# One product for numerators and denominators of tiles 8 to 15, a freer choice of engines, and smaller loads, in a planned transformer-block kernel

## The chip, the cores and the metric

The kernel runs on one core of one Trainium2 chip. A core has five engines that run their own instruction streams and meet at semaphores: TensorE (PE in the profile; PEld is its weight load), VectorE (DVE), ScalarE (ACT), GpSimd (POOL) and SyncE (SP), which here only issues DMAs. The metric is the device time of one execution in microseconds; the median of several executions is compared.

## The reference

One block with adaptive layer norms, an attention in linear form and a gated MLP, on 2048 tokens of width 512. What matters of it:

```python
def _A_ref(x, wqkv, w_phi, wo):           # 32 heads of 16
    pq, pk = q @ w_phi, k @ w_phi          # per head
    phi_q = concat([softmax(pq), softmax(-pq)])
    phi_k = concat([softmax(pk), softmax(-pk)])
    kv = einsum('bhsf,bhsd->bhfd', phi_k, v)
    z = einsum('bhsf->bhf', phi_k)
    num = einsum('bhqf,bhfd->bhqd', phi_q, kv)
    den = einsum('bhqf,bhf->bhq', phi_q, z)[..., None] + 1e-06
    return (num / den) @ wo
def _B_ref(x, w_gate, w_up, w_down):       # 1376 wide
    return (sigmoid(x @ w_gate) * (x @ w_up)) @ w_down
h = layernorm(x) * (1 + ca) + sa;  x = x + ga * _A_ref(h)
h = layernorm(x) * (1 + cb) + sb;  x = x + gb * _B_ref(h)
```

The six vectors sa to gb come from silu(c) @ w_mod.

## The kernel before, in words

The 2048 tokens are 16 tiles of 128. In the first part the kernel takes the statistics of every tile (bn_stats, L897 and L898), normalises it (xn, L923 to L927), transposes it on PE (tp_h, L941) or by a transposing DMA (L933), and applies the modulation (hm1, L948 and L950). K and V products (L968, L972) follow per tile; ScalarE takes exponentials of both signs (L984), VectorE sums and inverts them (L987, L1000), GpSimd multiplies (phi, L990), and PE adds phi times V into two accumulators (kvacc, L458). The column of ones in V makes the sums z beside kv. From the accumulators come block-diagonal matrices kvbd of 144 columns for each of 8 groups: 128 for the numerators, 8 for z and 8 for the plain sums of exponentials of the queries.

The second part works on units of one or two query tiles (UNITS). The queries' exponentials eT (L1047) lie transposed and not normalised. For a unit, sm (L553) multiplies eT by the last 16 columns of kvbd, 8 products a tile; smS (L557) copies half of the result, and den (L563 to L566) makes of it the factor cc for each head and sign. Then num (L578) multiplies eT by the first 128 columns, u (L584) scales it by cc, o (L602, GpSimd) adds the two signs, a DMA transposes o (L605), a_ps (L611) multiplies by wo. x1 (L616), its statistics (L620, L621), the second normalisation xn2 (L653 on ScalarE, L655 on VectorE), its transpose (L660) and mod (L675) give the input of the MLP. The MLP runs in chunks of 1, 1, 2, 4, 4 and 4 tiles: for each of 11 slices of the width a gate and an up product (L696), tg (tanh, L700, ScalarE) and hm (L705, VectorE), and then for each tile 11 products y (L719), fin (L728) and a store (L730).

The order is not the order of the program text. Every operation is a task in a graph, with the engines it may run on and their costs, its reads and writes, and its buffers. A list scheduler (order, L240) plays the graph through with these costs and always takes the ready task with the lowest due time; tables DUE, REL and ENG shift the due and release times of single tasks and fix engines. The result is one fixed order for each engine, with a wait wherever a task needs another's result or buffer. Buffers are rings with few places (CAPS, L424): 8 PSUM banks, 2 places for tg, 6 of 2 KB for phi and u, 2 for the inputs of an MLP chunk. Engines take their tasks strictly in the planned order.

Loads go through SP's queue, in planned order too: x in pieces of 2, 2, 4, 4 and 4 tiles (x0a, x0b, x1, x2, x3), the weights wk, wv, wq (512 KB each), w_mod in two pieces of 512 KB and one of 2 MB (wm1), wo, wg, wu, wd (L777 to L793). Before the first data come, PE runs 22 products on zeros (warm, L825).

A second graph behind a branch on a flag (L1124) repeats the work in a safer form for large inputs. With these inputs it is not taken.

Of the kernel before, what the change touches and what calls it, by code (L numbers as in the profile page):

```python
# [9 lines left out]
FP32 = mybir.dt.float32  # L10
# [6 lines left out]
P = 128  # L17
S, D, H, DH, F = 2048, 512, 32, 16, 1376
NT = S // P
KT = D // P  # L20
# [39 lines left out]
TD = [0, 0, 1, 0, 0, 0, 1, 1, 0]  # L60
DUE = {
    "ld_x0a": -97.1, "ld_wm01": 152.0, "ld_x0b": 222.2, "ld_wv": 207.5, "ld_x1": 81.5, "ld_x3": -0.1, "ld_wq": -14.2, "ld_wg": 19.9, "ld_wu": 3.4,
    "ld_wd": -29.9, "c1": 13.0, "c2": 147.3, "c3": 14.4, "scb": 6.0, "bd": 165.0, "pmem": 11.4, "wdz": -3.1, "modc1.0": 26.7, "modc1.1": 19.0,
    "modc1c": 2.7, "modc2.0": 74.4, "tpw0": -20.5, "wTc0": -4.8, "tpw1": -10.4, "wTc1": 7.4, "tpw2": 52.0, "wTc2": 2.1, "wTc3": 23.5, "foldc10": 219.5,
    "fold11": 191.9, "fold12": -0.3, "foldc12": -11.6, "fold13": -5.6, "foldc13": 5.3, "ld_wd2": 13.8, "wqT2": -3.5, "foldc00": -13.3, "fold01": 157.0,
    "foldc01": 0.1, "fold02": -52.2, "fold03": -1.9, "foldc03": 127.5, "st1_0": -0.5, "rs1_0": -0.3, "xn1_0": -6.5, "tph00": 49.2, "hm1_00": 5.6,
    "tph01": -4.8, "hm1_01": 155.9, "tph02": 63.8, "hm1_02": 82.7, "tph03": 34.8, "hm1_03": -1.8, "st1_1": -0.5, "nmr1_1": -5.4, "xn1_1": 112.1,
    "tph10": -23.9, "hm1_10": 3.2, "tph11": -0.8, "hm1_11": -7.3, "tph12": 28.2, "hm1_12": 97.5, "tph13": -14.9, "st1_2": 19.0, "st1_3": 33.1,
    "rs1_2": 32.5, "nmr1_2": 157.2, "xn1_2": -2.3, "xT1_2": 140.7, "xT1_3": 123.5, "hm1_20": 218.8, "hm1_21": -5.3, "hm1_22": -18.5, "hm1_23": -3.9,
    "st1_4": -3.5, "rs1_3": 79.1, "nmr1_3": -1.5, "xn1_4": 105.0, "xn1_5": -0.8, "tph30": -5.2, "hm1_30": -15.4, "tph31": -42.3, "hm1_31": -28.8,  # L70
    "tph32": 41.0, "hm1_32": 152.2, "tph33": -0.5, "hm1_33": 25.8, "st1_6": 162.7, "st1_7": 38.8, "rs1_4": 95.1, "nmr1_4": -2.5, "xn1_6": 219.0,
    "xn1_7": 209.9, "tph40": 160.1, "hm1_40": 104.8, "tph41": -30.3, "hm1_41": 90.7, "tph42": -16.0, "hm1_42": 9.7, "tph43": 140.8, "hm1_43": 56.3,
    "st1_8": -47.7, "st1_9": 172.5, "nmr1_5": 89.8, "tph50": 231.5, "hm1_50": -1.8, "hm1_51": 59.9, "tph52": 175.6, "hm1_52": 231.3, "tph53": -17.7,
    "hm1_53": -12.9, "st1_10": 18.2, "st1_11": 153.1, "rs1_6": -0.5, "nmr1_6": 0.5, "xn1_10": 91.7, "xT1_10": 127.3, "xT1_11": 123.6, "hm1_60": 29.7,
    "hm1_61": -1.0, "hm1_62": 199.8, "hm1_63": 6.2, "st1_12": -7.3, "st1_13": 11.8, "rs1_7": 10.0, "nmr1_7": -15.9, "xn1_12": 87.0, "xn1_13": -20.2,
    "xT1_12": 204.7, "xT1_13": -7.7, "hm1_70": -5.2, "hm1_71": -13.4, "hm1_72": -4.7, "hm1_73": 189.5, "st1_14": 106.3, "st1_15": -14.0, "rs1_8": 14.5,
    "nmr1_8": -9.3, "xn1_15": 108.4, "tph80": 17.5, "hm1_80": -4.7, "tph81": 15.4, "hm1_81": -25.1, "tph82": 14.9, "hm1_82": -4.7, "tph83": 98.2,
    "hm1_83": -4.7, "K0": -4.8, "e0.0": 17.5, "n0.0": 92.8, "r0.0": -1.1, "V0": 141.0, "kv0.0": 14.6, "K1": -21.7, "e1.0": 155.4, "n1.0": 12.9,
    "r1.0": -29.0, "va1": 5.5, "kv1.0": -3.5, "K2": -3.7, "e2.0": -26.5, "n2.0": 5.8, "r2.0": 0.9, "phi2.0": 90.9, "V2": 40.0, "va2": 61.0, "kv2.0": 17.6,
    "K3": -10.3, "e3.0": 141.6, "n3.0": -16.1, "r3.0": -4.1, "phi3.0": 192.3, "V3": 21.9, "va3": 8.8, "kv3.0": -13.1, "K4": 34.7, "e4.0": 10.3,  # L80
    "r4.0": -19.6, "phi4.0": 69.5, "V4": 129.0, "kv4.0": 68.3, "K5": 158.4, "e5.0": -6.7, "n5.0": -0.2, "r5.0": 182.5, "phi5.0": 7.9, "V5": 156.3,
    "va5": 209.5, "kv5.0": 68.4, "K6": 1.8, "e6.0": 11.3, "n6.0": -3.5, "r6.0": -9.4, "phi6.0": 217.5, "V6": 1.0, "va6": 23.6, "kv6.0": -7.7, "K7": -26.2,
    "e7.0": -7.2, "n7.0": -8.8, "r7.0": 27.6, "phi7.0": 32.4, "V7": -6.3, "va7": 99.3, "kv7.0": -15.3, "K8": 2.3, "e8.0": -17.2, "n8.0": 104.1,
    "r8.0": 17.0, "phi8.0": -6.8, "V8": -3.5, "va8": 42.1, "kv8.0": 6.7, "K9": 152.5, "n9.0": -40.0, "r9.0": -2.9, "phi9.0": 87.3, "V9": 0.3, "va9": -14.4,
    "kv9.0": -1.4, "e10.0": 2.6, "n10.0": 83.9, "V10": -10.5, "va10": -24.9, "K11": -1.8, "e11.0": -20.5, "n11.0": 0.3, "r11.0": -2.4, "phi11.0": 8.5,
    "e11.2": 35.6, "r11.2": -38.9, "n11.4": -6.0, "phi11.4": -0.3, "e11.6": -16.4, "r11.6": 248.2, "phi11.6": 5.2, "V11": -11.2, "va11": 131.5,
    "kv11.0": 4.3, "kv11.4": 25.6, "kv11.6": 0.7, "K12": -47.6, "e12.0": -5.7, "r12.0": 0.6, "phi12.0": 28.5, "V12": 22.2, "kv12.0": 0.7, "K13": 0.2,
    "n13.0": 31.7, "r13.0": -2.9, "phi13.0": 11.3, "n13.4": 9.9, "r13.4": -5.2, "phi13.4": 8.1, "V13": 83.3, "va13": 72.9, "kv13.0": 79.9, "kv13.4": -6.7,
    "K14": 83.3, "e14.0": -6.3, "n14.0": 106.6, "r14.0": 116.9, "e14.4": -4.5, "n14.4": 6.8, "r14.4": 0.5, "V14": 161.0, "va14": -8.2, "kv14.0": -20.6,
    "kv14.4": -8.1, "K15": 107.4, "e15.0": 0.1, "n15.0": 0.8, "r15.0": -0.7, "phi15.0": 4.0, "e15.4": -2.9, "n15.4": 0.7, "phi15.4": 8.5, "va15": 60.4,  # L90
    "kv15.0": 78.1, "kv15.4": 15.7, "perm": 45.8, "kvm0": 186.2, "kvm1": -4.0, "kvp0": 3.0, "kvp1": 22.2, "kvp2": -20.5, "kvz0": 67.0, "kvz1": -5.4,
    "kvn1": 119.1, "kvz2": -16.9, "gbc": -29.4, "ga": -9.7, "gac": -2.9, "wo0": -30.7, "wo1": 79.0, "wo2": -42.3, "wo3": -21.1, "wmod_free": 122.0,
    "wd0": -0.5, "wd1": 0.3, "wd2": -0.5, "wd3": 90.8, "wd4": 29.9, "wd5": 0.2, "wd6": 28.7, "wd7": 11.0, "wd9": 7.6, "wd10": 6.8, "Q00": 111.8,
    "qe00": -26.3, "Q01": -2.5, "qe01": 62.0, "Q02": -19.2, "qe02": -2.3, "Q03": 168.0, "Q10": 91.7, "qe10": -13.7, "Q11": 76.2, "qe11": -27.8,
    "Q12": 10.0, "qe12": 86.0, "Q13": -0.5, "qe13": 5.1, "Q20": 2.0, "qe20": 60.8, "qe21": 14.0, "qe22": 106.1, "Q23": -11.0, "qe23": 13.1, "Q30": 78.8,
# [111 lines left out]
class Graph:  # L207
# [948 lines left out]
```

## Time and profile before

| | us |
|---|---|
| median of 9 runs | 220.72 (220.44 to 221.67) |
| profiled execution | 221.19 |
| its span | 219.3 |
| last VectorE operation begins | 213.68 |

The span runs from the first to the last instruction; about 1.9 us of the execution lie around it. In the groups of instructions, "mean ns" is the time of one instruction from start to end. Neighbours on one engine can overlap, so a row of equal instructions takes less than the sum of the means: 16 sm products have a mean of 169 ns each, and follow each other in 24. Therefore the spacing of starts on the timeline is used for PE and VectorE where it is known.

The costliest groups of the part that the change touches:

```profile
L584 DVE TENSOR_TENSOR u<-num,cc 128x512 f32<-128x512 f32 x28 | 18.2, 682 | 0.9 <-PE num L578 0.5
...
L602 POOL TENSOR_TENSOR o<-u 128x512 bf16<-128x512 f32 x14 | 17.5, 1267 | 48.4 <-DVE u L584 35.9 <-ACT tg L700 12.4
...
L578 PE MATMUL num<-kvbd,eT 128*128 128x128 bf16 x128 | 10.4, 219 | 0.0
...
L675 DVE TENSOR_SCALAR wT_sb<-wT_sb,modc 128x256 bf16<-128x256 bf16 x16 | 4.5, 339 | 0.5 <-DMA wT_sb<-xn 0.4
...
L553 PE MATMUL sm<-kvbd,eT 128*128 128x16 bf16 x128 | 4.3, 169 | 0.0
```

The columns after the bar are busy us, mean ns of one, and the idle time of the engine just before, with what ended it.

### The profile page before, as it was taken

How to read it: one execution, taken by the hardware profiler on the slowest of the kernel's cores; microseconds unless marked ns; L12 is line 12 of the kernel's file. 1: busy time of each engine (PE TensorE's matmuls, PEld its weight loads, DVE VectorE, ACT ScalarE, POOL GpSimd, SP SyncE). 2: the span in 40 equal slices, each digit the busy share in tenths (PEclk: the TensorE clock that was granted, in tenths of full speed). 3: DMA queues.
4: the chain of work that ended last, by engine and by line, in shares of the span. 5: the costliest groups of instructions: out<-in, count | busy, mean ns of one | idle time of the engine just before them, and what ended most of it. 6: DMA issues, size and time to landing. Idle time of an engine off the chain costs nothing.

```text
span 219.3 us, 4340 instructions
## 1 busy us (share of the span) xinstructions
PE 205.4 (94%) x1583; PEld 114.7 (52%) x1583; DVE 165.3 (75%) x381; ACT 109.0 (50%) x255; POOL 89.9 (41%) x113
## 2 busy tenths in 40 slices
PE   7986989999899989999999999998999999999990
PEld 2733545464466568867775454553454444444450
DVE  3989899998469998878969777899698854344230
ACT  3789898999769974523630532240332522332100
POOL 4249898999999944521102015340006100000000
PEclk9996999999999999999999999999999999999997
DMA  6995995991000201250431003054002322000021
GB/s 188 364 243 138 334 216 109 346 379 48 0 3 0 43 16 22 49 98 0 51 72 48 27 1 72 1 75 120 0 24 51 72 51 72 0 4 0 27 72 34
DMA packets 31455, 19.02 MB, mean 87 GB/s; under 512 B 21729, under 2 KB 29378, under 8 KB 31426
## 3 DMA queue, kind: packets, MB, share of 16 engines
q1 hardware_dynamic: 30896, 18.65, 33.6%
q8 instruction: 14, 0.23, 0.4%
q14 instruction: 15, 0.12, 0.2%
q10 hardware_dynamic: 530, 0.02, 0.1%
HBM read 11.58 MB, written 2.10 MB: 62 GB/s over the span
## 4 chain that ended last, share of the span: by engine, by line
PE 66%; DMA 12%; DVE 8%; ACT 4%; SPq 3%; POOL 2%; issue 2%; ACTq 0%; POOLq 0%; DVEq 0%
PE u_ps L696 17%; PE g_ps L696 17%; PE y_ps L719 14%; DMA wqk_sb<-in_A_wqkv_dram 5%; PE a_ps L611 4%; PE k_ps L968 4%; PE v_ps L972 3%; DVE u L584 2%; PE num L578 2%; DMA wp_sb<-in_A_w_phi_dram 2%; DMA wqk_sb<-xn 2%; ACT e L984 2%; DMA x_sb<-in_A_x_dram 2%; POOL phi L990 2%; SPq L660 1%
## 5 line engine op out<-in xcount | busy, mean ns | idle before, releaser
L700 ACT ACTIVATE tg<-g_ps 128x512 bf16<-128x512 f32 (+4 forms) x66 | 29.6, 454 | 73.2 <-PE g_ps L696 64.2
L705 DVE SCALAR_TENSOR_TENSOR wmod_sb<-tg,u_ps 128x512 bf16<-128x512 bf16 (+5 forms) x66 | 32.4, 503 | 23.0 <-PE u_ps L696 20.4
L719 PE MATMUL y_ps<-wd_sb,wmod_sb 128*128 128x512 bf16 (+3 forms) x187 | 42.8, 366 | 0.0
L602 POOL TENSOR_TENSOR o<-u 128x512 bf16<-128x512 f32 x14 | 17.5, 1267 | 48.4 <-DVE u L584 35.9
L696 PEld LDWEIGHTS <-wu_sb 128*128 128x128 bf16 (+1 forms) x264 | 23.3, 100 | 17.7 <-issue 0.6
L696 PEld LDWEIGHTS <-wg_sb 128*128 128x128 bf16 (+1 forms) x264 | 23.2, 100 | 17.1
L990 POOL TENSOR_TENSOR phi<-e,ks 128x1024 bf16<-128x1024 bf16 (+2 forms) x22 | 31.5, 1452 | 0.3
L719 PEld LDWEIGHTS <-wmod_sb 128*128 128x128 bf16 (+1 forms) x187 | 17.8, 98 | 15.7
L696 PE MATMUL u_ps<-wT_sb,wu_sb 128*128 128x512 bf16 (+3 forms) x132 | 26.0, 326 | 0.0
L696 PE MATMUL g_ps<-wT_sb,wg_sb 128*128 128x512 bf16 (+3 forms) x132 | 25.5, 326 | 0.0
L696 PE MATMUL u_ps<-wqk_sb,wu_sb 128*128 128x256 bf16 (+5 forms) x132 | 21.3, 290 | 0.3 <-DVE x L616 0.3
L584 DVE TENSOR_TENSOR u<-num,cc 128x512 f32<-128x512 f32 (+1 forms) x32 | 20.7, 682 | 1.0 <-PE num L578 0.5
L696 PE MATMUL g_ps<-wqk_sb,wg_sb 128*128 128x128 bf16 (+5 forms) x132 | 21.2, 290 | 0.0
L987 DVE TENSOR_REDUCE ks<-e 128x64 f32<-128x1024 bf16 (+2 forms) x22 | 19.3, 912 | 0.8 <-ACT e L984 0.8
L728 DVE TENSOR_TENSOR ot<-y_ps,x 128x512 bf16<-128x512 f32 (+1 forms) x17 | 11.1, 656 | 9.8 <-PE y_ps L719 9.6
L984 ACT ACTIVATE e<-k_ps 128x512 bf16<-128x512 f32 (+2 forms) x44 | 18.3, 491 | 0.4 <-PE k_ps L968 0.2
L972 PE MATMUL v_ps<-wv_sb,h1T 128*128 128x512 bf16 x64 | 17.2, 400 | 0.7 <-DVE h1T L950 0.7
L611 PE MATMUL a_ps<-wo_sb,oT 128*128 128x512 bf16 x64 | 16.3, 379 | 1.1 <-DMA oT<-o 1.0
L1047 ACT ACTIVATE eT<-q_ps 128x512 bf16<-128x512 f32 x32 | 16.9, 626 | 0.2 <-PE q_ps L1042 0.2
L968 PE MATMUL k_ps<-wqk_f,h1T 128*128 128x512 bf16 x64 | 16.0, 379 | 0.0
L1042 PE MATMUL q_ps<-h1T,wqk_f 128*128 128x512 bf16 x64 | 15.6, 379 | 0.0
L897 DVE BATCH_NORM_STATS2 st<-x_sb 128x6 f32<-128x512 bf16 x16 | 10.8, 673 | 4.0 <-DMA x_sb<-in_A_x_dram 4.0
(129 smaller groups left out, 276.8 us busy)
## 6 DMA issues: line engine op xcount, KB each, us to landing
wmod_sb<-in_w_mod_dram SPq DMA_DIRECT2D x1, 2048.0 KB, 10.4
out_dram<-ot SPq DMA_DIRECT2D x15, 128.0 KB, 1.7
x_sb<-in_A_x_dram SPq DMA_DIRECT2D x3, 512.0 KB, 6.6
wg_sb<-in_B_w_gate_dram SPq DMA_DIRECT2D x1, 1376.0 KB
wu_sb<-in_B_w_up_dram SPq DMA_DIRECT2D x1, 1376.0 KB, 9.6
wd_sb<-in_B_w_down_dram SPq DMA_DIRECT2D x1, 1280.0 KB, 13.6
wqk_sb<-in_A_wqkv_dram SPq DMA_DIRECT2D x2, 512.0 KB, 7.6
wmod_sb<-in_w_mod_dram SPq DMA_DIRECT2D x2, 512.0 KB, 6.4
```

Source lines behind the costliest of these rows:

```text
L584: dve.tensor_tensor(u[:], ps[:].rearrange("p (h d) -> p h d", d=DH), cc[:, q, s, :].unsqueeze(2).to_broadcast([P, H, DH]), op=ALU.mult)
L602: G.add(f"o{t}", {"POOL": 1.3}, lambda e, ub=ub, o=o: pool.tensor_tensor(o[:], ub[0][:].rearrange("p h d -> p (h d)"), ub[1][:].rearrange( ...
L611: pe.matmul(ap_[:], lhsT=oT[:, j, :], rhs=wo_sb[:, j, :], start=(j == 0), stop=(j == KT - 1))
L696: pe.matmul(ps[:fsz, 0:n], lhsT=w[:, j, ft * P:ft * P + fsz], rhs=h[:, j, 0:n], start=(j == 0), stop=(j == KT - 1))
L700: G.add(f"tg{k}.{ft}", {"ACT": 0.13 + n * 0.00083}, lambda e, tg=tg, g_ps=g_ps, fsz=fsz, n=n: act.activation(tg[:fsz, 0:n], g_ps[:fsz, 0:n ...
L705: dve.scalar_tensor_tensor(hm_all[:fsz, hm[k].slot, ft, 0:n], tg[:fsz, 0:n], 1.0, u_ps[:fsz, 0:n], op0=ALU.add, op1=ALU.mult)
L719: pe.matmul(y[:, 0:c1 - c0], lhsT=hm_all[:fsz, hm[k].slot, ft, tl * P:(tl + 1) * P], rhs=wd_sb[:fsz, ft, c0:c1], start=(ft == 0), stop=(ft ...
L968: pe.matmul(kp[:], lhsT=h1T[:, j, t * P:(t + 1) * P], rhs=wqk_f[:, j, D:2 * D], start=(j == 0), stop=(j == KT - 1))
L972: pe.matmul(vp[:], lhsT=h1T[:, j, t * P:(t + 1) * P], rhs=wv_sb[:, j, :], start=(j == 0), stop=(j == KT - 1))
L984: act.activation(ee[:, ha:hb, s, :], kp[:, ha * DH:hb * DH].rearrange("p (h j) -> p h j", j=DH), ACT.Exp, scale=1.0 - 2.0 * s)
L987: dve.tensor_reduce(ks[:, ha:hb].rearrange("p h s -> p (h s)"), ee[:, ha:hb].rearrange("p h s j -> p (h s) j"), axis=AX.X, op=ALU.add)
L990: pool.tensor_tensor(ph[:, ha * 32:hb * 32].rearrange("p (h j) -> p h j", j=DH), ee[:, ha:hb].rearrange("p h s j -> p (h s) j"), ks[:, ha: ...
```

## The change

It has four parts.

1. For units 5 to 8 (tiles 8 to 15; MGU = 5) the products sm and num become one product with all 144 columns of a group. A tile's 8 groups fill three PSUM banks (groups 0 to 2, 4 to 6, and 3 with 7). Three copies z take the 16 last columns of each group to SBUF, on ScalarE or VectorE; dn makes cc from them, and u is cut in four pieces for each tile. A tile's numerators wait for the cc of the tile before.
2. The planner may choose among more engines: copies between ScalarE and VectorE, o, wo and wd between GpSimd and VectorE, xn2 and mod among three engines. A preference keeps the old engine except where the table ENG names another. In the built order 48 tasks change engine: among them 16 mod tasks leave VectorE (12 to ScalarE, 4 to GpSimd), four xn2 go from ScalarE to GpSimd and one (tile 14) to VectorE, and hm1_71 goes from GpSimd to VectorE.
3. The third piece of w_mod is loaded as three (512 KB, 1 MB, 512 KB), and loads are released at other times. SP's order at the start becomes x0a, wk, x0b, the two w_mod pieces, x1, wv, wq, x2, two transposes, one transpose of wq, x3 (before: x0a, wk, x0b, the two w_mod pieces, wv, x1, x2, wq, two transposes, two transposes of wq, x3).
4. DUE, REL and ENG are new throughout, so the order of all engines is new.

```diff
+            merged = p >= MGU
+            if merged:
+                for q, t in enumerate(tiles):
+                    zS = small("smS", [P, 8, 16])
+                    for i in range(3):
+                        ps = nums[t, i] = bank("num")
+                        gs = range(4 * i, 4 * i + 3) if i < 2 else (3, 7)
+                        def f_num(e, t=t, gs=gs, ps=ps):
+                            for c, g in enumerate(gs):
+                                pe.matmul(ps[:, c * (P + 16):(c + 1) * (P + 16)], lhsT=eT[t // 4][:, g, (t % 4) * P:(t % 4 + 1) * P],
+                                          rhs=kvbd[:, g, :], start=True, stop=True)
...
+                        G.add(f"num{t}{i}", {"PE": 0.0615 * len(gs)}, f_num, r=KVZ + [("kvn", 0), ("kvn", 1), ("kvn", 2), ("cc", t - 1)] + eTk, w=[("num", t, i)],
...
+                        G.add(f"z{t}{i}", {"ACT": 0.24, "DVE": 0.13}, f_z, r=[("num", t, i)], w=[("z", t, i)], bufs=[ps, zS], due=d0 + q, pref=["ACT"])
+                    def f_small(e, zS=zS, m=m, den=den, cc=cc):
+                        zv = zS[:].rearrange("p (s b) n -> p s b n", s=2)
+                        for s in range(2):
+                            dve.tensor_tensor(m[:, 0, s * 32:(s + 1) * 32].rearrange("p (b n) -> p b n", n=8),
+                                              zv[:, s, :, 0:8], zv[:, 1 - s, :, 8:16], op=ALU.mult)
+                        dve.tensor_tensor(den[:, 0], m[:, 0, 0:32], m[:, 0, 32:64], op=ALU.add)
+                        dve.reciprocal(den[:, 0], den[:, 0])
+                        for s in range(2):
+                            dve.tensor_tensor(cc[:, 0, s].rearrange("p (b n) -> p b n", n=8), zv[:, 1 - s, :, 8:16],
+                                              den[:, 0].rearrange("p (b n) -> p b n", n=8), op=ALU.mult)
...
+                    for i in range(3):
+                        for s in (i,) if i < 2 else (0, 1):
+                            nh, h0, c0 = (24, 0, 0) if i < 2 else (8, 24, s)
...
-    load("wm1", ["wmod1"], lambda e: sp.dma_start(wmod_sb[:, :, 1024:3072], wmod_v[:, :, 1024:3072]), 2048 * K1, 30.0, rel=22.0)
+    for nm, c0, c1, due in (("ga", 2, 3, LD[1]), ("m2", 3, 5, LD[2]), ("gb", 5, 6, LD[3])):
+        load("wm" + nm, ["wmod_" + nm], lambda e, c0=c0, c1=c1: sp.dma_start(wmod_sb[:, :, c0 * D:c1 * D], wmod_v[:, :, c0 * D:c1 * D]), (c1 - c0) * 512 * K1, due, rel=due)
...
-                G.add(f"mod{p}{j}", alts, f_mod, r=rr, w=[("h2", p, j)], bufs=bb, due=d0 + 3, port=() if via_pe else ("DVE",))
+                    pf, alts, rr, bb = ["DVE"], {"DVE": 0.27, "ACT": 0.47, "POOL": 0.45}, [("h2raw", t) for t in tiles] + ["mod2"], [h2[k]]
+                G.add(f"mod{p}{j}", alts, f_mod, r=rr, w=[("h2", p, j)], bufs=bb, due=d0 + 3, port=() if via_pe else ("DVE", "POOL"), pref=pf)
```

The f_small here is the dn task: two products, one sum, one reciprocal and two products, six operations of 32 columns.

## The prediction

> **What bounds the kernel now.** I read the page first (shares of the engines and the 40 slices), then windows of 5 us, then the timeline where a window loses time.
>
> ```profile
> span 219.3 us, 4340 instructions
> ...
> PE 205.4 (94%) x1583; PEld 114.7 (52%) x1583; DVE 165.3 (75%) x381; ACT 109.0 (50%) x255; POOL 89.9 (41%) x113
> ...
> PEclk9996999999999999999999999999999999999997
> ```
>
> PE is the bound. The reader should see two things: PE's 6% of idle time and the one dip of the clock in the fourth slice. The windows (columns: stretch, its length, busy time of PE, PEld, DVE, ACT, POOL with counts, granted clock, DMA share, GB/s) say where they lie:
>
> ```profile
> 15.00:20.00 5.00, 2.10 (x13) 0.83 (x12) 4.90 (x14) 3.73 (x11) 4.13 (x5) 0.85 0.55 86
> 20.00:25.00 5.00, 5.00 (x32) 2.52 (x31) 4.12 (x13) 4.24 (x13) 4.21 (x5) 0.81 0.89 243
> ...
> 40.00:45.00 5.00, 5.00 (x44) 2.59 (x42) 4.97 (x7) 5.00 (x11) 4.94 (x9) 1.00 1.03 412
> ...
> 55.00:60.00 5.00, 4.44 (x51) 2.54 (x49) 2.41 (x5) 3.85 (x11) 4.84 (x5) 1.00 0.00 0
> ...
> 115.00:120.00 5.00, 5.00 (x40) 2.51 (x39) 4.63 (x11) 0.43 (x2) 1.27 (x1) 1.00 0.14 40
> ...
> 150.00:155.00 5.00, 3.96 (x19) 1.67 (x18) 3.65 (x8) 0.60 (x1) 0.00 (x0) 1.00 0.38 92
> ```
>
> PE idles 2.9 us at 15 to 20 and works at half clock just after, 0.6 at 55 to 60, 1.0 at 150 to 155; between, 5.00 of 5.00. At 30 to 55 VectorE, ScalarE and GpSimd are full too. The timeline shows what the two large gaps wait for:
>
> ```profile
> 12.73 0.69 DVE L897 BATCH_NORM_STATS2 st<-x_sb 128x6 f32<-128x512 bf16 x1 [0.79 <-DMA x_sb<-in_A_x_dram]
> ...
> 17.05 0.23 PE L941 MATMUL tp_h<-ident,xn 128*128 128x128 bf16 x1 [1.64 <-POOL xn L927]
> ...
> 19.11 1.89 PE L972 MATMUL v_ps<-wv_sb,h1T 128*128 128x512 bf16 x4 [0.75 <-DVE h1T L950]
> ```
>
> ```profile
> 151.85 1.04 PE L611 MATMUL a_ps<-wo_sb,oT 128*128 128x512 bf16 x4 [1.04 <-DMA oT<-o]
> ```
>
> The first is a chain: tokens 512 to 1023 (load x1) land, VectorE takes their statistics, GpSimd normalises, PE transposes. The second is one output product waiting for a transposed o behind SP's queue. The four v matmuls at 19.11 take 1.89 us; four take 0.86 elsewhere in the chain of waits.
>
> **What the Trainium skill says.** "TensorE: Matmul & The Clock Gate", part 1, states that an idle window of 3413 ns halves the clock; here the dip lasts one such window (0.85 and 0.81 granted), so the trace agrees. The same page, "Wait — 56ns, not 53.3ns?", gives a floor of about 25 ns from start to start for small matmuls: the sm products show 0.39 us for 16. "DMA: Bandwidth & Descriptors", [...]its HWDGE ordering part say that one queue's descriptors are consumed in order, so a load moved forward in SP's list lands earlier by the bytes it overtakes. "SBUF — State Buffer", the shared port pair, says that GpSimd and some VectorE forms lock each other out; a VectorE xn at 5.83 us took 1.23 us beside a GpSimd operation, 0.38 at 8.58, which agrees.
>
> **The change, part by part.** Durations are from the profiled execution (span 219.3, its own time 221.19, so 1.9 us lies around the span); the median is 220.72. I apply differences to the median.
>
> 1. One product for tiles 8 to 15. Before, each tile costs PE 8 sm and 8 num products:
>
> ```profile
> 113.01 0.39 PE sm L553 x16
> ...
> 114.06 0.45 PE num L578 x8
> ```
>
> That is 24.4 and 56.2 ns each, 0.645 us a tile. After: 8 products of 144 columns at 56.2 x 144/128 = 63 ns (estimate from the row), 0.506 us. Eight tiles: -1.1 us of PE, in a stage where PE is full. Bounds: -0.8 if short products were partly hidden, -1.5 if 144 columns cost no more than 128.
>
> 2. What it costs VectorE. Before, a pair's den takes from 117.60 to 119.03 on the timeline, 1.43 us, and u 0.60 us from start to start (three in 1.88), four per pair: 1.92 us a tile. After: six small operations on 32 columns. Independent tiny ones follow each other in 0.08 us and dependent ones in 0.19 (timeline at 155.3 to 156.0), a 32-column reciprocal takes 0.353 (group L565): about 1.1. Then u of 384 elements twice (0.47 each, 0.60 scaled, against 0.425 busy for the 256-column ot) and of 128 twice (0.21): 1.36. Together 2.46, +0.54 a tile, +4.3 in all. Six of the 24 z copies go to VectorE (about 0.15 each, +0.9), and xn2 of tile 14 (0.804 mean, +0.7). ScalarE gets 18 z copies at about 0.21 (smS 128x64) against 1.8 us of smS; it is 50% busy, so this is hidden. Against it, 16 mod operations leave VectorE: 0.28 each (eight in 2.22 us), -4.4. Net +1.5 over the kernel, but about +4 inside 115 to 175, where the windows hold 51.4 busy of 60. That fits, at 92%, if it is spread evenly. Bounds for PE: 0 to +0.5 us for each tile. The numerators of a tile now wait for the denominator of the tile before (cc of t-1), and queued behind them on PE are y and gate products; in the built order 2.4 us or more of other PE work (counted at 0.86 us for four products of 512 columns and 0.216 for one) lies between consecutive tiles, against about 3.2 us of VectorE work per tile, fins included. I take +0.3 in all.
>
> 3. Loads. x1 is issued before wv, wq before x2, x3 behind one transposed load instead of two; the 2 MB w_mod load is cut in three. x1 overtakes 512 KB: at the 330 GB/s of window 10 to 15 that is 1.6 us, so it lands near 11.2 instead of 12.7, and wv there instead of 11.2 (7.8 us from its issue). VectorE is free at 11.9, so the statistics of tiles 4 and 5 gain 0.8, and the normalisation after them (two more statistics stand ahead of nmr) about 1.2. The first V product needs wv at 13.31: cover 0.6 us; if that is gone, the same 1.2 is lost again. x2 lands 1.6 us later, near 17, and VectorE reads it after 18. The later w_mod pieces are needed after 40 us; cutting them costs SP two issues of 0.57, between transposes that have slack. Earlier transposes on PE: 1.2 of the 2.9 us.
>
> 4. Engines. In the key stage GpSimd's work from 43.86 is one unbroken run, and its last phi releases PE:
>
> ```profile
> 43.86 16.34 POOL L990 TENSOR_TENSOR phi<-e,ks 128x1024 bf16<-128x1024 bf16 x14
> ```
>
> One hm1 leaves it (0.555). On ScalarE, two fold copies, an hm1 and the two-part reciprocals go to VectorE, while va7, va12 and va13 come: -1.1 us up to the last e. VectorE in exchange gains about +1.4 up to its last reciprocal; its cover is the start, 0.8 to 1.2 earlier, and the 0.77 it waits for ScalarE at 53.95. So the stage can end 1.2 + 0.5 sooner by GpSimd; with VectorE nearly used up I take -1.5 for parts 3 and 4 together (bounds 0 and -2.2).
>
> 5. New order near 150. In the built order tile 12's transposed o stands before y's last 22 products (4.7 us), and needs about 4 (POOL o 1.27, SP issue, 2.4 to landing). The 1.04 gap goes; late next are the modulations of tiles 8 to 11, so -0.7. The tail (last y to end, 5.6 us) keeps its form: a full store before the last half one; 0, at most +0.2. The switch of other copies between ScalarE and VectorE has cover on both: 0.
>
> Sum: -1.1 + 0.3 - 1.5 - 0.7 = -3.0; 220.72 - 3.0 = 217.7.
>
> **Rivals.** (a) The start's gain stays in the start: VectorE, with +1.4 us, ends the key stage where it did, and PE idles at 57 to 60 instead of 16 to 19. For it: 4.97 of 5.00 VectorE at 40 to 45; against: 2.41 at 55 to 60. Then -1.1 + 0.3 - 0.7: 219.2. (b) PE's activity in the window before 18.5 grows enough that the clock is not halved. For: the transposes come 1.2 us earlier; against: even then PE works only some 1.2 of that 3.4 us. The 3.4 us at half speed cost 1.7: 216.0. (c) Slower: the chain product, z copy, small operations, u per tile is longer than the PE work laid between tiles, so PE's in-order queue stands at each tile's numerators, and banks (three per tile instead of two and a shared half) come free late, which holds gate and up products too. Price per tile t; it turns the sign from 3.3/8 = 0.41 us a tile, and at 0.55 gives 220.72 - 3.3 + 4.4 = 221.8. For: VectorE at 92% and six small operations in a row; against: the mods that leave, and PE without idle time from 115 to 150 today. (d) Everything comes out even: 220.7.
>
> **Numbers.** Forecast 217.7 (own range 216.6 to 218.8) 0.47; (a) 219.2 (218.8 to 220.2) 0.16; (b) 216.0 (215.2 to 216.6) 0.14; (c) 221.8 (220.9 to 223) 0.17; (d) 220.7 0.06. A change within 0.2% (0.44 us) can't be told from none: faster 0.47 + 0.16 + 0.14 = 0.77, same 0.06, slower 0.17. The range leaves out most of (c) and the lower end of (b): 215.4 to 220.9.
>
> **What would show it.** Sm products drop from 128 to 64 and num rows show 144 columns at about 63 ns; the first tp_h of tile 4 near 15.9 and a shorter PE gap; the phi run on POOL ending near 58.6; no gap over 0.4 us before out12; PE idle at 115 to 150 under 0.7 us. It is wrong if PE shows waits on dn or u of tiles 8 to 15 of more than 3 us in sum, if V's first product waits for wv, or if VectorE rather than GpSimd ends the key stage.

## The result, and the profile after

| | before | after |
|---|---|---|
| median of the runs, us | 220.72 | 219.48 |
| lowest to highest | 219.83 to 221.67 (31 runs) | 218.86 to 219.98 (10 runs) |
| profiled execution, us | 221.19 | 219.67 |
| its span | 219.3 | 217.9 |
| last VectorE operation begins | 213.68 | 211.87 |

The ratio is 0.9946, with a 95% interval of 0.993 to 0.9962: faster by 0.54%, 1.2 us. The forecast was 217.7, 3.0 us faster. The sign held, and 219.48 lies inside the widest range that was given (215.4 to 220.9), but outside the forecast's own (216.6 to 218.8): 1.8 us of the expected gain is missing. The page of the kernel after begins:

```profile
span 217.9 us, 4268 instructions
...
PE 205.5 (94%) x1519; PEld 113.7 (52%) x1519; DVE 168.7 (77%) x425; ACT 111.0 (51%) x268; POOL 95.8 (44%) x121
...
PEclk9997999999999999999999999999999999999999
```

The totals look like those of before: PE 94% again, one dip of the clock in the same slice. What changed is where PE idles, so the windows of 5 us are read next (same columns as before: stretch, length, PE, PEld, DVE, ACT, POOL, clock, DMA share, GB/s):

```profile
15.00:20.00 5.00, 3.21 (x17) 1.27 (x16) 4.90 (x14) 4.73 (x12) 3.98 (x5) 0.90 0.73 140
20.00:25.00 5.00, 5.00 (x29) 2.38 (x27) 4.68 (x15) 4.00 (x13) 5.00 (x6) 0.76 1.08 305
...
55.00:60.00 5.00, 4.71 (x71) 3.09 (x69) 2.98 (x8) 3.83 (x9) 4.92 (x6) 1.00 0.01 3
...
110.00:115.00 5.00, 4.81 (x34) 2.59 (x32) 4.79 (x17) 2.22 (x8) 0.30 (x1) 1.00 0.08 28
115.00:120.00 5.00, 4.12 (x26) 2.06 (x24) 4.76 (x16) 1.44 (x4) 1.90 (x2) 1.00 0.21 53
120.00:125.00 5.00, 3.89 (x19) 1.65 (x17) 4.90 (x10) 0.60 (x1) 3.12 (x3) 1.00 0.26 52
150.00:155.00 5.00, 5.00 (x25) 2.25 (x23) 4.07 (x17) 0.60 (x1) 0.00 (x0) 1.00 0.27 56
```

The gap at 15 to 20 shrank from 2.9 to 1.8 us and the one at 150 to 155 from 1.0 to nothing. In their place PE idles at 115 to 125, where it worked 5.00 of 5.00 before: 2.0 us in these two windows. This is the stretch in which tiles 8 to 11 pass through the new product and dn. VectorE is nearly full there, and GpSimd is busy with o.

Why VectorE is late there is seen in its own timeline (start, duration, operation). The first four lines are the dn of tile 8, the next line comes from that of tile 10, the last three from that of tile 11:

```profile
108.57 0.29 DVE L660 TENSOR_TENSOR m<-smS 128x32 f32<-128x32 f32 x2 [0.34 <-ACT smS L650]
108.90 0.19 DVE L662 TENSOR_TENSOR den<-m 128x32 f32<-128x32 f32 x1
109.13 0.35 DVE L663 RECIPROCAL den<-den 128x32 f32<-128x32 f32 x1
109.52 0.29 DVE L665 TENSOR_TENSOR cc<-smS,den 128x32 f32<-128x32 f32 x2
...
115.35 1.38 DVE L660 TENSOR_TENSOR m<-smS 128x32 f32<-128x32 f32 x2
...
119.54 1.14 DVE L662 TENSOR_TENSOR den<-m 128x32 f32<-128x32 f32 x1
120.72 0.35 DVE L663 RECIPROCAL den<-den 128x32 f32<-128x32 f32 x1
121.11 0.90 DVE L665 TENSOR_TENSOR cc<-smS,den 128x32 f32<-128x32 f32 x2
```

The same operations take 0.29, 0.19 and 0.29 us in tile 8, and 1.38, 1.14 and 0.90 later: 1.09 + 0.95 + 0.61 = 2.65 us more. The reciprocal between them, with one input, keeps its 0.35. GpSimd's timeline for the same time:

```profile
115.32 1.27 POOL L743 TENSOR_TENSOR o<-u 128x512 bf16<-128x512 f32 x1 [5.02 <-DVE u L710]
119.37 2.49 POOL L743 TENSOR_TENSOR o<-u 128x512 bf16<-128x512 f32 x2 [2.79 <-DVE u L710]
```

The m at 115.35 ends at 116.73, just after the o that began at 115.32 has ended at 116.59. Of the two o at 119.37 to 121.86, the sum den waits for the end of the first, and cc for the end of the second. And PE stands behind them:

```profile
113.61 0.89 PE L643 MATMUL num<-kvbd,eT 128*128 128x144 bf16 x8
114.63 1.04 PE L841 MATMUL g_ps<-wT_sb,wg_sb 128*128 128x512 bf16 x4
...
118.39 0.55 PE L643 MATMUL num<-kvbd,eT 128*128 128x144 bf16 x6 [0.88 <-DVE u L710]
...
122.65 1.02 PE L841 MATMUL g_ps<-wT_sb,wg_sb 128*128 128x512 bf16 x4 [1.11 <-DVE u L710]
```

The numerators of tile 11 wait 0.88 us, and a gate product queued behind the next bank 1.11. In brackets stands u, since it releases the bank; u itself is late by dn.

The time in brackets counts each of these waits about 0.16 us short, because the modelled end of a product lies behind the usual start of the next one (a product of 512 columns is drawn as 0.38 us long, but the next starts after 0.216). Counted from start to start, as what lies between two neighbours beyond the usual distance for the shape, the two waits are 1.04 and 1.28 us. Tile 10's numerators lose another 0.52: their eight products take 1.02 us, from 113.61 to the next product at 114.63, in place of 0.50. An up product at 163.25 loses 0.37 to a late u. Together that is 3.2 us between 105 and 165, and it is called PE's loss below. The kernel before, counted in the same way, loses 1.2 there, all of it in its gap at 150.

### The profile page after: what moved, and what is told of

The parts are those of the page before. It is cut to its first block, busy times and chain, and to the rows that moved or that the text cites. A ratio compares the mean times of both kernels' runs of the same rounds, so it can differ in the third digit from the quotient of the medians.

```text
span 217.9 us, 4268 instructions
## 1 busy us (share of the span) xinstructions
PE 205.5 (94%) x1519; PEld 113.7 (52%) x1519; DVE 168.7 (77%) x425; ACT 111.0 (51%) x268; POOL 95.8 (44%) x121
## 4 chain that ended last, share of the span: by engine, by line
PE 68%; DVE 12%; ACT 6%; DMA 4%; issue 3%; POOL 3%; SPq 1%; DVEq 0%; POOLq 0%; ACTq 0%
PE g_ps L841 16%; PE y_ps L864 16%; PE u_ps L841 15%; PE a_ps L752 6%; PE q_ps L1188 4%; DVE ks L1133 3%; ACT e L1130 2%; POOL phi L1136 2%; DMA wqk_sb<-in_A_wqkv_dram 2%; PE v_ps L1118 2%; ACT h1T L1094 2%; PE num L719 2%; DMA h1T<-xn 2%; PE k_ps L1114 2%; DVE u L710 1%
## 5 line engine op out<-in xcount | busy, mean ns | idle before, releaser
L845 ACT ACTIVATE tg<-g_ps 128x512 bf16<-128x512 f32 (+3 forms) x66 | 29.4, 454 | 58.6 <-PE g_ps L841 35.0
L864 PE MATMUL y_ps<-wd_sb,wmod_sb 128*128 128x512 bf16 (+3 forms) x187 | 42.3, 367 | 0.0
L841 PE MATMUL u_ps<-wT_sb,wu_sb 128*128 128x512 bf16 (+3 forms) x132 | 25.2, 326 | 0.0
L841 PE MATMUL u_ps<-wqk_sb,wu_sb 128*128 128x128 bf16 (+5 forms) x132 | 20.8, 290 | 0.2 <-DVE u L710 0.2
L841 PE MATMUL g_ps<-wqk_sb,wg_sb 128*128 128x128 bf16 (+5 forms) x132 | 20.6, 290 | 0.0
L1118 PE MATMUL v_ps<-wv_sb,h1T 128*128 128x512 bf16 x64 | 16.7, 390 | 1.0 <-DVE h1T L1096 0.7
L1114 PE MATMUL k_ps<-wqk_f,h1T 128*128 128x512 bf16 x64 | 16.7, 394 | 0.0
L1177 POOL TENSOR_TENSOR wd_sb<-wd_sb,wmod_sb 128x512 bf16<-128x512 bf16 x11 | 12.6, 1173 | 0.0
```

Source lines behind the costliest of these rows:

```text
L841: pe.matmul(ps[:fsz, 0:n], lhsT=w[:, j, ft * P:ft * P + fsz], rhs=h[:, j, 0:n], start=(j == 0), stop=(j == KT - 1))
L845: G.add(f"tg{k}.{ft}", {"ACT": 0.13 + n * 0.00083}, lambda e, tg=tg, g_ps=g_ps, fsz=fsz, n=n: act.activation(tg[:fsz, 0:n], g_ps[:fsz, 0:n ...
L864: pe.matmul(y[:, 0:c1 - c0], lhsT=hm_all[:fsz, hm[k].slot, ft, tl * P:(tl + 1) * P], rhs=wd_sb[:fsz, ft, c0:c1], start=(ft == 0), stop=(ft ...
L1114: pe.matmul(kp[:], lhsT=h1T[:, j, t * P:(t + 1) * P], rhs=wqk_f[:, j, D:2 * D], start=(j == 0), stop=(j == KT - 1))
L1118: pe.matmul(vp[:], lhsT=h1T[:, j, t * P:(t + 1) * P], rhs=wv_sb[:, j, :], start=(j == 0), stop=(j == KT - 1))
```

## The experiments

Two theories for the missing 1.8 us.

Theory L, a lock: a VectorE operation with two inputs from SBUF and a GpSimd operation that reads SBUF shut each other out for a whole instruction. The Trainium skill, "SBUF — State Buffer", in its part on the shared port pair, says so: whichever starts first "gets the pair for the whole instruction; the other fully blocks". The merge moved the factors of dn's products from PSUM and SBUF to SBUF alone, and it made dn's sum, a reduce of one input before, a sum of two inputs in SBUF. So it brought both under this lock. The times above agree; that it is the cause was to be shown.

Theory W, work: dn has six operations a tile in place of four for two tiles, VectorE is full, and its mere length holds PE up.

The ratios are to the kernel before, measured beside each set (its medians were 220.61, 220.77 and 220.58). The last column is PE's loss between 105 and 165 us in the profiled execution, counted from start to start; it is 3.2 in the kernel after and 1.2 in the kernel before. The edits below are shown shortened.

| run | us | ratio, 95% interval | PE's loss, us |
|---|---|---|---|
| e1_dn_from_psum | 217.90 | 0.9882 (0.9858 to 0.9905) | 1.5 |
| e2_o_four_pieces | 217.92 | 0.9873 (0.9853 to 0.9893) | 1.9 |
| e3_wv_first | 219.77 | 0.9966 (0.9947 to 0.9984) | 3.2 |
| e4_o_on_dve | 217.42 | 0.9852 (0.9829 to 0.9875) | 1.4 |
| c_after_again | 219.54 | 0.9958 (0.9942 to 0.9974) | 3.2 |
| e5_hm1_71_pool | 219.75 | 0.9958 (0.9942 to 0.9975) | 3.2 |
| e6_before_dn_sbuf | 223.92 | 1.0141 (1.0111 to 1.017) | 1.2 |
| e7_o_dve_y14_first | 217.79 | 0.9869 (0.984 to 0.9897) | 1.4 |
| c_e4_again | 217.40 | 0.9852 (0.983 to 0.9873) | 1.3 |
| e8_psum_and_o_dve | 218.48 | 0.9903 (0.9883 to 0.9923) | 2.4 |
| e9_all_o_dve | 217.22 | 0.9848 (0.9827 to 0.987) | 1.3 |

**e1: dn without two SBUF inputs.** Of each product in dn one factor is read from the PSUM bank, and the sum becomes a reduction with one input. That takes ten operations in place of six.

```diff
-dve.tensor_tensor(m[s], zv[s][0:8], zv[1 - s][8:16], op=ALU.mult)
-dve.tensor_tensor(den, m[0:32], m[32:64], op=ALU.add)
+for b0, b1, src in pz(s, 0):          # src: PSUM, three blocks or one
+    dve.tensor_tensor(m[s, b0:b1], src, zv[1 - s, b0:b1, 8:16], op=ALU.mult)
+dve.tensor_reduce(den, m as (h, s), axis=AX.X, op=ALU.add)
...
+    dve.tensor_tensor(cc[s, b0:b1], src, den[b0:b1], op=ALU.mult)
```

> The planned order is kept; only the operations inside dn change. One factor of each product of dn is read from PSUM instead of SBUF, and the sum is a reduce of one input, so no VectorE operation of dn has two inputs in SBUF any more; dn has 10 operations instead of 6 (about +0.2 us a tile). Theory L (lock): in the changed kernel the m of tile 10 (1.38 us for two) and the sum and cc of tile 11 (1.14 and 0.90) stood behind GpSimd's o because two SBUF inputs need the port pair that GpSimd holds, 2.65 us in sum, and PE's gaps at 117 and 122 (0.88 and 1.11 us) follow from it. Then no operation of dn takes over 0.5 us, PE idle at 110 to 125 falls from 2.2 to under 1 us, and the time falls by 1 to 2 us, to 217.5 to 218.5. Theory W (work): VectorE has too much to do in this stretch (4.8 of 5 us busy) whatever blocks it. Then 8 tiles with 0.2 us more each make it slower, 220 to 221, and the gaps stay or grow.

Measured: 217.90, 1.6 us below the kernel after, with more operations. From VectorE's timeline of this kernel, the dn of tile 11, and from GpSimd's the o beside it:

```profile
118.41 0.42 DVE L664 TENSOR_TENSOR m<-num,smS 128x24 f32<-128x24 f32 x4
118.86 0.22 DVE L666 TENSOR_REDUCE den<-m 128x32 f32<-128x64 f32 x1
119.12 0.35 DVE L667 RECIPROCAL den<-den 128x32 f32<-128x32 f32 x1
119.50 0.42 DVE L670 TENSOR_TENSOR cc<-num,den 128x24 f32<-128x24 f32 x4
```

```profile
118.57 2.50 POOL L748 TENSOR_TENSOR o<-u 128x512 bf16<-128x512 f32 x2 [1.82 <-DVE u L715]
```

The products m begin 0.16 us ahead of the first o; the rest lies inside the two o (118.57 to 121.07), and nothing waits: m and cc take 0.42 each, as in tile 8 (108.55, 0.42). L holds, and W, which has more operations cost more, falls as the main cause.

**e2: o in four pieces.** The same o of tiles 8 to 15 as four GpSimd operations of 128 columns, so that a lock lasts a quarter as long.

```diff
-o[:] = u0[:] + u1[:]
+for a in range(0, D, D // 4): o[:, a:a + D // 4] = u0[:, a:a + D // 4] + u1[:, a:a + D // 4]
```

> The planned order is kept. GpSimd's o of tiles 8 to 15 (1.27 us) is cut in four operations of 128 columns (about 0.4 us each, 1.6 in sum); VectorE's work is unchanged. L: a blocked operation of dn waits for one piece instead of for the rest of 1.27 us, so m, sum and cc lose at most 0.4 us each; PE idle at 110 to 125 falls under 1.2 us; 218.0 to 218.8. If GpSimd takes the port again at once for its next piece, no gain. W: VectorE has the same work, so 219.5, and o lands 0.3 us later.

Measured: 217.92. GpSimd needs longer (1.69 us for four pieces, 1.27 for one), and the m that took 1.38 takes 0.89, the den 0.34 in place of 1.14, the cc 0.81 in place of 0.90. The m and the cc each lose more than the 0.4 that was expected, since each is two products and both can wait for a piece; the time came out just below the expected range all the same. GpSimd works longer and the kernel is faster, so what counts is the length of its single instruction, not its work.

**e4: o off GpSimd.** o of tiles 8 to 11 goes to VectorE, in the same place of the order. That adds about 0.6 us a tile to the fullest engine.

```diff
+if t.name in ("o8", "o9", "o10", "o11"): t.eng = "DVE"
```

> The planned order is kept, but o of tiles 8 to 11 runs on VectorE in its place (about 0.65 us each, +2.6 us of VectorE work in the stretch) and GpSimd is free there. L: no operation of dn is stretched (-2.65 us on VectorE), so VectorE ends the stretch where it did or slightly earlier: 218.8 to 219.6. W: 2.6 us more work on a full engine: 221.5 to 222.

Measured: 217.42, faster than either theory expected. L had set the work of o on VectorE against the waits that go, but PE's loss shows that this work cost PE only about 0.5 us. VectorE's timeline shows the operations of tiles 10 and 11 back at 0.28, 0.19 and 0.29; the windows show PE nearly without idle time at 115 to 125:

```profile
115.36 0.28 DVE L660 TENSOR_TENSOR m<-smS 128x32 f32<-128x32 f32 x2
...
119.06 0.19 DVE L662 TENSOR_TENSOR den<-m 128x32 f32<-128x32 f32 x1
...
119.68 0.29 DVE L665 TENSOR_TENSOR cc<-smS,den 128x32 f32<-128x32 f32 x2
```

```profile
20.00:25.00 5.00, 4.36 (x38) 2.21 (x36) 4.86 (x15) 4.67 (x15) 5.00 (x6) 1.00 1.09 299
...
115.00:120.00 5.00, 4.89 (x30) 2.39 (x28) 4.69 (x21) 1.44 (x4) 0.00 (x0) 1.00 0.16 44
120.00:125.00 5.00, 5.00 (x24) 2.20 (x23) 5.00 (x10) 0.65 (x2) 0.00 (x0) 1.00 0.18 35
```

The two orders are equal, so the same instruction can be dated in both. m of tile 8 begins at 108.57 after and 108.58 here; the first m of tile 13 at 142.73 and 141.02; that of tile 14 at 153.53 and 151.70; the last VectorE operation at 211.87 and 210.04. The difference is 0.0, 1.71, 1.83 and 1.83: with the work of o on VectorE already paid, taking away the lock at tiles 10 and 11 is worth 1.83 us of the profiled execution (2.1 by the medians), and nearly all of it before tile 13.

**e6: the lock put into the kernel before.** The only edit is that den's two products take both factors from SBUF; for that, ScalarE's copy smS carries twice the columns, which takes 0.37 us a pair in place of 0.27.

```diff
-act.copy(smS[:, 0:nt], sm[:, 0:nt, 64:128])
-dve.tensor_tensor(m[:, 0:nt], sm[:, 0:nt, 0:64], smS[:, 0:nt], op=ALU.mult)
+act.copy(smS[:, 0:nt], sm[:, 0:nt, 0:128])
+dve.tensor_tensor(m[:, 0:nt], smS[:, 0:nt, 0:64], smS[:, 0:nt, 64:128], op=ALU.mult)
...
+dve.tensor_tensor(cc, smS[:, 0:nt, 64:128], den, op=ALU.mult)
```

> The kernel before, with only this edit: the copy smS takes all 128 columns of a pair's sums to SBUF, and den's two products read both factors from there instead of one from PSUM. If two SBUF inputs are locked out by a GpSimd operation on SBUF (theory L), the one den that stands beside an o (m at 117.60, o from 117.16 to 118.43) waits until about 118.4, so its m takes 1.0 to 1.2 us in place of 0.28, and the dens at 108.15, 119.03 and 157.05, which stand beside no o, keep 0.28; PE is full there with little cover, so the time rises by 0.2 to 0.8. If the length of dn comes from the number of its operations or from VectorE's load alone (theory W), all dens keep 0.28 and the time stays within 0.2.

Measured: 223.92, slower by 1.4%, 3.1 us. VectorE's timeline:

```profile
64.71 1.21 DVE L563 TENSOR_TENSOR m<-smS 128x64 f32<-128x64 f32 x1
...
68.37 0.97 DVE L563 TENSOR_TENSOR m<-smS 128x128 f32<-128x128 f32 x1
...
78.36 1.15 DVE L566 TENSOR_TENSOR cc<-smS,den 128x128 f32<-128x128 f32 x1
...
120.40 0.98 DVE L563 TENSOR_TENSOR m<-smS 128x128 f32<-128x128 f32 x1
...
122.54 0.28 DVE L563 TENSOR_TENSOR m<-smS 128x128 f32<-128x128 f32 x1
```

The one beside an o (119.96 to 121.23) takes 0.98, and the ones that stand alone keep 0.28: as L said. The size was wrong by far, because the expectation looked only at o. The first three stand beside the operations with which GpSimd folds gates into wo and wd, a long run and a single one (78.20 to 79.36):

```profile
64.66 6.94 POOL L1031 TENSOR_TENSOR wd_sb<-wd_sb,wmod_sb 128x512 bf16<-128x512 bf16 x6
```

There m waits for up to one of these operations, 1.16 us each, and PE, which has little else to do at the start of the second part, works 3.74 and 4.47 of 5.00 us at 65 to 75 in place of 5.00 and 5.00. The den at 108.15 in the kernel before begins at 110.95 here, so 2.80 us are lost by then; at the last VectorE operation the lag is 2.84. The wait beside the o at 120 thus cost nothing at the end, though the expectation priced it at 0.2 to 0.8: PE's loss from 105 on is that of the kernel before. The folds of wd shut VectorE out as o does, and what a wait costs depends on whether VectorE stands on the path there. This is the strongest showing of L: one factor moved from PSUM to SBUF in a kernel that is otherwise unchanged, but for the copy that is 0.1 us longer.

**c_e4_again, e8 and e9: is it one gain, and is there more of it?**

> The kernel with o of tiles 8 to 11 on VectorE once more, as partner for the next two: 217.2 to 217.7, ratio to before 0.983 to 0.987.

e8 puts e1 and e4 together:

> Both cures together: o of tiles 8 to 11 on VectorE and dn's products with one factor from PSUM. Theory L: each takes away the same lock, so the gains don't add; within 0.3 of the kernel with o on VectorE alone, 217.2 to 217.8. If they work by separate means (fewer waits of dn on the one hand, an earlier o on the other), the gains add: 220.72 x 0.9852 x 0.9882 / 0.9946, about 216.0.

e9 is e4 for all of tiles 8 to 15:

```diff
-if t.name in ("o8", "o9", "o10", "o11"): t.eng = "DVE"
+if t.name in ("o8", "o9", ..., "o15"): t.eng = "DVE"
```

> o of all tiles 8 to 15 on VectorE. In the profile of the changed kernel no dn of tiles 12 to 15 stands beside an o (their products take 0.28 to 0.29 us), so theory L expects no further gain: within 0.3 of the kernel with only tiles 8 to 11 moved, or slower by up to 0.5 where VectorE's 0.6 us more per tile comes in front of hm. If o on GpSimd costs by its own length (theory W's other half: 1.27 us there against about 0.6), the gain of tiles 8 to 11 comes again, 0.5 or more.

Measured: 217.40, 218.48 and 217.22. e9 can't be told from e4 (0.9848 and 0.9852), as L expected: tiles 12 to 15 had no dn beside an o. e8 missed: the gains don't add, but nor does the pair stay at 217.4; it is 1.1 us slower than e4. No lock is left in its timeline. Its dn takes 1.47 us (109.05 to 110.52) in place of 1.33 (108.71 to 110.04), 0.14 more for each of eight tiles, and the o too are on VectorE, which is busy 4.86 to 4.93 of each 5.00 us at 110 to 125. PE's loss rises from 1.3 to 2.4, which is the 1.1 us. So W is right in its place: once VectorE is full to the brim, its mere length counts. The longer dn had its price in e1 too, which is 0.5 us behind e4: PE loses 0.13 us at 143 and 0.25 at 153 there, where e4 loses nothing.

**e3: the load x1 behind wv again.**

```diff
+i, j = at["ld_x1"], at["ld_wv"]
+order[i], order[j] = order[j], order[i]
```

> The planned order is kept but for one exchange on SP: wv is issued before x1 again, as in the kernel before. By the prediction's part 3, x1 ahead is worth 1.2 us at the first transposes of tile 4: 220.7. By the trace of the changed kernel, where VectorE begins x1's statistics at 12.04 without waiting and K starts 0.7 us later than before, it is worth 0.7: 220.2. If the start's gain is lost before the key stage ends (rival a): 219.5, with the last phi ending at the same 58.3.

Measured: 219.77, 0.2 to 0.3 above the kernel after by the medians; the intervals overlap, so by the time alone it can't be told from it. Its timeline:

```profile
12.95 0.69 DVE L1043 BATCH_NORM_STATS2 st<-x_sb 128x6 f32<-128x512 bf16 x1 [0.87 <-DMA x_sb<-in_A_x_dram]
...
17.27 0.23 PE L1087 MATMUL tp_h<-ident,xn 128*128 128x128 bf16 x1 [1.28 <-POOL xn L1073]
```

The wait for x1 is back (0.87), and the transpose of tile 4 begins at 17.27 in place of 16.34. Of these 0.9 us, 0.5 reach the end of the key stage in the profiled execution (the last phi of the run ends at 58.84 in place of 58.35) and stay to the last VectorE operation (212.37 in place of 211.87). So the gain of the start is lost in part before the key stage ends, which is rival (a) in small.

**c_after_again and e5: the clock, and hm1_71 back on GpSimd.**

> The changed kernel once more, unaltered, beside the others: 219.2 to 219.8, ratio to before 0.993 to 0.996. It gives the other three a partner on the same chip.

> The changed kernel with hm1_71 on GpSimd again (the fourth part undone for this one operation). The prediction's step 4 expects the phi run to end 0.55 us later (58.9 in place of 58.3) and the time to rise by 0.4 to 0.6, to 219.9 to 220.1. Rival: VectorE, which gets 0.4 us back, or ScalarE ends the stage; then the phi run ends at 58.3 to 58.5 all the same and the time stays within 0.2 of the changed kernel.

```diff
+if t.name == "hm1_71": t.eng = "POOL"
```

Measured: 219.54 and 219.75, with the same ratio. The step that the prediction priced at 0.5 shows 0.2 by the medians and nothing by the ratios. One reason may be that GpSimd in the kernel after waits 0.18 us for VectorE's sums at 40.71, ahead of the long phi run, so that part of the operation taken off it had cover; no run shows this alone. The expected date of the phi run's end can't be checked, because the clock differs: in the profiled execution of e5 the run ends at 59.54, with a granted clock of 1.00 at 15 to 20 and 0.66 at 20 to 25.

The profiled execution of c_after_again is of use for another question, the clock:

```profile
15.00:20.00 5.00, 2.07 (x12) 0.82 (x12) 4.89 (x12) 3.59 (x10) 3.36 (x5) 0.79 0.72 180
20.00:25.00 5.00, 5.00 (x23) 2.35 (x22) 4.40 (x11) 3.69 (x11) 5.00 (x6) 0.52 1.07 300
```

Here the clock is down for about twice as long as after, and the phi run (GpSimd, 45.06 for 14.49 us) ends at 59.55 in place of 58.35, 1.2 us later. At 20 to 25 the clock was halved for about 4.8 us here (0.52), for 3.4 us in e5 (0.66) and for 2.4 us after (0.76), each worked out from the granted clock. In e5 this was one stretch as long as the one of after, only later, and the phi run ended as late as here; so where the stretch falls counts, though e5's additional operation on GpSimd can have added up to 0.56. In e4 it isn't down at all (1.00 in the window at 20, shown there), and PE is simply idle 0.64 us in that window.

**e7: the tail.** e4 with the full tile 14 ahead of both halves of tile 15.

```diff
+# among the y, fin and st tasks of tile 14 and the first half of tile 15: tile 14 first
+part.sort(key=lambda t: t.name.split(".")[0])
```

> The best version so far (o of tiles 8 to 11 on VectorE, 217.42) with the full tile 14 finished and stored before both halves of tile 15, as the tail stood in the kernel before. If the two stores that stand together on SP's queue at the end make the tail longer (last VectorE operation to end 5.86 there, 5.62 before), it falls to 5.4 to 5.65 and the time by 0.2 to 0.4, to 217.0 to 217.2. If the half store alone sets the end, the time stays within 0.15 of 217.4.

Measured: 217.79, no gain; its last VectorE operation begins at 210.10, 6.0 us before the end of its span. The order of the stores makes no difference that shows.

The merged product alone, in the order of before, wasn't tried.

## Why the prediction was wrong in size, step by step

Step 1, the product: right. Eight products of 144 columns begin at 110.09, and the y product queued behind them at 110.59: 0.50 us a tile, 62 ns each, where 63 and 0.506 were estimated.

```profile
110.09 0.66 PE L643 MATMUL num<-kvbd,eT 128*128 128x144 bf16 x8
110.59 2.33 PE L864 MATMUL y_ps<-wd_sb,wmod_sb 128*128 128x512 bf16 x10
```

Against 0.645 that is 1.2 us for eight tiles.

Step 2, what the merge costs VectorE and through it PE: this is the term that failed, "I take +0.3 in all". PE's loss at the merged tiles is 3.2 us; the prediction's own sign, PE idle under 0.7 us at 115 to 150, reads 2.0. The prediction took VectorE's chain as covered by PE's other work; in fact PE stood for 1.04 and 1.28 us behind dn of tiles 10 and 11, where VectorE waited for o. In e4, without the lock, 1.4 us are left, so taking it away is worth 1.8 of the 3.2, as the dates say too. About 0.5 of the 1.4 comes with the work of o on VectorE (waits at 118, 121 and 126 that e1 doesn't have). The other 0.9 (tile 10's numerators and the product at 163.25) stands in e4 as it stands after; there PE waits for VectorE, and VectorE's own length fits it: dn undisturbed takes 1.35 us (108.57 to 109.92), not 1.1. That dn's length makes these 0.9 us is not shown, since no run shortened it; e8 shows only that more length adds to them. The price of u was right, 0.67 us for two pieces, 1.34 a tile, against 1.36, and so was that of a dependent operation: "VectorE: DVE Perf Modes" of the Trainium skill, in the part on the TRN2 errata, gives (N + 151) / 0.96 ns for an fp32 tensor_tensor at 512 and 2048 columns; carried to 32 columns that is an estimate of 191 ns, and the trace shows 0.19.

The loss was partly hidden by gains that the prediction priced too low or not at all. It read PE as working "5.00 of 5.00" between its gaps, but the kernel before has these windows too:

```profile
60.00:65.00 5.00, 4.74 (x74) 3.20 (x75) 3.22 (x14) 2.97 (x9) 5.00 (x6) 1.00 0.02 3
...
75.00:80.00 5.00, 4.46 (x38) 2.60 (x37) 4.90 (x13) 4.57 (x10) 2.36 (x4) 1.00 0.26 53
...
95.00:100.00 5.00, 4.68 (x44) 3.31 (x43) 3.96 (x12) 0.94 (x3) 1.27 (x1) 1.00 0.36 58
```

In the kernel after they read 4.98, 4.97 and 5.00. From start to start that is a gain of 0.9 us. With it the sum comes out: 1.85 at the end of the key stage, 0.9 here, 1.2 by the product and 1.2 at 150, less 3.2, makes 1.9; VectorE's last operation moved forward by 1.81. By the prediction's own sum, which has 3.3 us of gain without this term, a loss of 3.2 would have left next to nothing. That the sign held is in part luck.

The text had the two things that would have led there. It named the shared port pair and gave a trace of it (an xn of 1.23 us in place of 0.38), but only for the start. It had 3.2 us of VectorE work a tile against 2.4 us of PE work between tiles, which is rival (c)'s condition, and still took 0.3. What it didn't ask is where the operands of dn now lie: its products moved from PSUM and SBUF to SBUF alone, its sum now has two inputs there, and an o of an earlier tile can stand beside them, as it did in tiles 10 and 11.

Step 3, the loads, and step 4, the engines: the sum was nearly right, 1.85 us at the end of the phi run (60.20 to 58.35) against 1.5, and the parts were not. x1 ahead of wv gives 0.5 there (e3), hm1_71 about 0.2 of the whole time, if anything (e5). The other 1.1 or more are left to the new order and the other engine choices, which weren't undone one by one. The reading behind step 4 was off as well: the run from 43.86 holds phi alone, so hm1_71 could not leave it; it stood ahead of it. In the kernel after, the phi run that begins at 43.89 holds 13 operations instead of 14; one more was done before it:

```profile
43.89 14.46 POOL L1136 TENSOR_TENSOR phi<-e,ks 128x1024 bf16<-128x1024 bf16 x13
```

The transpose of tile 4 comes at 16.34, where 15.9 was expected:

```profile
12.04 0.68 DVE L1043 BATCH_NORM_STATS2 st<-x_sb 128x6 f32<-128x512 bf16 x1
...
16.34 0.23 PE L1087 MATMUL tp_h<-ident,xn 128*128 128x128 bf16 x1 [0.31 <-POOL xn L1073]
```

The statistics gained the 0.7 that were free (12.73 to 12.04, now without a wait for the load); the 1.2 for the normalisation weren't reached.

Step 5: right in kind, and more than it was priced. The output product of tile 12 begins at 150.06 without a wait, the gap of 1.04 is gone, and nothing came late in its place; 0.7 was taken.

```profile
150.06 1.03 PE L752 MATMUL a_ps<-wo_sb,oT 128*128 128x512 bf16 x4
```

The tail was 6.0 us from the last VectorE operation in the profiled execution, and 5.6 before, where 0 to 0.2 more was set. But it varies from execution to execution, from 5.5 to 5.9 in the other runs of this order, and e6, in the order of before, has 5.9. So no difference of the tail is shown.

Rivals: (a) is refuted, since the key stage ended 1.85 sooner. (b) had its price wrong: a clock that isn't halved gains nothing measurable (e1, e2 and e4 have 1.00 at 15 to 25, and their phi runs end within 0.2 us of the kernel after). (c) is what took place, mostly in two tiles of eight: the chain through VectorE was longer than PE's cover, for a reason that it didn't name. It cost 3.2 us in sum, just under the 3.3 from which the sign turns by that sum.

## What to carry to other kernels

When an operand moves from PSUM to SBUF, look up on the timeline which GpSimd operations will stand beside its reader: a short VectorE operation with two SBUF inputs may then last as long as a whole GpSimd instruction, and a chain of them can wait more than once, as dn of tile 11 did. One factor left in PSUM together with a one-input form of the sum, or GpSimd's operation moved to VectorE, took the wait away here, even though VectorE's busy time grew. A single input alone is no safe sign: the fp32 reduce and reciprocal kept their length beside an o, but the bf16 xn of one input that the prediction quotes took 1.23 us beside a GpSimd operation. Then ask whether VectorE stands on the path there: in e6, waits of this kind cost 2.8 us in sum at the start of the second part, and the one at 120 cost nothing. And count VectorE's length next: with VectorE busy for 97% of a stretch (e8), 0.14 us more a tile showed as 1.1 us in the total.

## What the runs showed of the hardware

- VectorE waits for GpSimd by whole instructions: a 128x32 sum that takes 0.19 us took 1.14 beside the first of two o (2.49 together), and the products after the reciprocal took 0.90 in place of 0.29 beside the second. Beside GpSimd's folds of wd it was the same (m 1.21 in e6). Four products with one factor in PSUM took 0.42 both alone and beside a running o. The reverse, an o that waits for VectorE, isn't seen: in the kernel after every o took 1.26 to 1.28.
- Moved to VectorE, an o took 0.68 us, against 1.27 on GpSimd.
- The halved clock moves from run to run. The Trainium skill, "TensorE: Matmul & The Clock Gate", part 1, calls the window free-running, and the runs agree: with the same program it was down for one window, for two, or not at all in the start. Of 22 executions of the kernel after (c_after_again), the five with a mean granted clock of 0.977 to 0.979 took 220.2 to 221.3 us; of the 17 from 0.983 to 0.997, all but one (220.9) took 219.06 to 219.74, without a trend. The profiles say where it hurts. Halved up to about 22.4 us, it cost nothing that shows (phi run to 58.35 after, to 58.2 in e1, e2 and e4 at full clock), since PE waits for data there even at full clock (0.64 us at 20 to 25 in e4). Halved up to about 24.8, it went with a phi run that ended 1.2 us later.
